# Attention and a two-layer network on one core: every product in 64x64 quarters of the matmul array, in an order worked out by a planner

## The chip, the core and the metric

The kernel runs on one core of a Trainium2 chip. A core has five engines with a queue each: TensorE (PE, matmuls; PEld is its weight load), VectorE (DVE), ScalarE (ACT), GpSimd (POOL) and SyncE (SP, which here only issues DMAs). They share the on-chip memory (SBUF, 128 partitions) and meet through semaphores; matmuls write to PSUM, eight banks of 512 f32 columns. Each engine takes its own instructions strictly in the order in which they were built. The metric is the device time of one execution in microseconds (us). The kernel before took 422.13 us, the median of two runs (421.86 and 422.4). A difference of about 2% is what counts as faster or slower here.

## The reference

Eight batches, twelve heads, 448 tokens, 64 channels a head; then a network of 768 -> 2048 -> 768 over the 3584 tokens.

```python
q_n, k_n = rmsnorm(q, g_q), rmsnorm(k, g_k)       # (8, 12, 448, 64)
scores = q_n @ k_n.T / sqrt(64);  attn = softmax(scores)
x = (attn @ v).transpose(0, 2, 1, 3).reshape(3584, 768)
out = gelu_tanh(x @ w_in) @ w_out                 # 768 -> 2048 -> 768
```

Inputs and output are f32; the kernels compute the products in bf16 with f32 sums.

## The kernel before

Per batch the work has a front (squares of q and k, their sums, one over the root, the normed tiles, a transpose to put channels on partitions), the attention, layer 1 and layer 2. Work of three batches runs at once: while batch b's scores and exponentials are made, layer 2 of earlier batches fills TensorE, and in layer 1 of batch b the front of batch b+1 runs on the other engines.

- **Scores** (`scores`, L300): for a pair of heads and 128 keys, one matmul a head, 64 rows by 128 columns of the array, the two heads side by side on the two row halves; the two outputs lie in two neighbouring PSUM banks, so that **one ACTIVATE (L326) takes the exponential of both heads, 896 columns**, with a per-partition bias `shift`. 448 keys are three blocks of 128 and a rest of 64; the rests of two pairs share one tile in four 64x64 matmuls (L310). A batch has 21 such tiles and so 21 exponentials.
- **Sums and products** (`pair_products`, L345): 128 rows by 64 columns, two heads on the two column halves. The rest block uses V tiles half filled with zeros (`vr`). DVE adds the exponentials of the key blocks (`key_sum`) before the sum product, and turns the sums into reciprocals (`recip_in`, `recip`, `recip_out`) and scales (`pair_x`).
- **Layer 1** (`mm1`) and **layer 2** (`mm2`): 128 rows by 64 columns, the two column halves one after the other (`parts=2`); the first batch's layer 1 and the last layer 2 tiles use the whole 128x128 array.
- **Front**: q is loaded with 4 tokens a partition on 112 partitions, k with 3 tokens a partition on 128 and a rest on 64. Transposes go through TensorE in the first batch and part of the second, later through DMA.

The order is written by hand: a string of steps for the first batch (`FRONT`, L737), and for the others lists of what comes after which group of layer 1 (`plan`, `first_blocks`) and how many layer 2 matmuls stand between two groups of scores (`FILLS`).

Of the kernel before, what the change touches and what calls it, by code (L numbers as in the profile page):

```python
# [12 lines left out]
AX = mybir.AxisListType  # L13


@with_exitstack
def kernel(
# [21 lines left out]
    P = 112  # L39
    NQ = S // P  # L40
    NK = 3
    NS = 7
    HP = H // 2
    CH = 4
    NCH = H // CH
# [3 lines left out]

    consts = ctx.enter_context(tc.tile_pool(name="consts", bufs=1))  # L50
    wts = ctx.enter_context(tc.tile_pool(name="wts", bufs=1))
    rawqk = ctx.enter_context(tc.tile_pool(name="rawqk", bufs=4))
    sqp = ctx.enter_context(tc.tile_pool(name="sqp", bufs=4))
    stp = ctx.enter_context(tc.tile_pool(name="stp", bufs=2))
    smp = ctx.enter_context(tc.tile_pool(name="smp", bufs=4))
    nrmp = ctx.enter_context(tc.tile_pool(name="nrmp", bufs=2))
    qkp = ctx.enter_context(tc.tile_pool(name="qkp", bufs=1))
    exq = ctx.enter_context(tc.tile_pool(name="exq", bufs=3))
    exr = ctx.enter_context(tc.tile_pool(name="exr", bufs=2))
    xp = ctx.enter_context(tc.tile_pool(name="xp", bufs=2))  # L60
    gp = ctx.enter_context(tc.tile_pool(name="gp", bufs=1))
    op = ctx.enter_context(tc.tile_pool(name="op", bufs=3))

    spots = [
        ctx.enter_context(tc.tile_pool(name=f"ps_s{i}", bufs=1, space=bass.MemoryType.PSUM))
        for i in range(2)
    ]
    unused, taken = [0, 1], []
    ps_o = ctx.enter_context(tc.tile_pool(name="ps_o", bufs=1, space=bass.MemoryType.PSUM))
    ps_m = ctx.enter_context(tc.tile_pool(name="ps_m", bufs=1, space=bass.MemoryType.PSUM))  # L70

    ps_t = tc.tile_pool(name="ps_t", bufs=1, space=bass.MemoryType.PSUM)
    ps_t_tiles = ps_t.__enter__()
# [5 lines left out]

    zeros = consts.tile([128, S], BF16)  # L80
    nc.vector.memset(zeros, 0.0)
    grow = consts.tile([D, 2], F32)
    for i, row in enumerate((g_q, g_k)):
        nc.scalar.dma_start(grow[:, i:i + 1], row.rearrange("(d o) -> d o", o=1))
    EXP_SET, GELU_SET = "natural_log_exp_and_others", "gelu_apprx_tanh_and_others"

# [5 lines left out]
    eps = consts.tile([128, 1], F32)  # L92
    win = wts.tile([128, HP, d_ff], BF16)
    wout = wts.tile([128, nf, d_model], BF16)

    vb = [wts.tile([128, H, NK, D], BF16, name=f"vb{i}") for i in range(2)]
    vr = [wts.tile([128, 2, HP, D], BF16, name=f"vr{i}") for i in range(2)]
    ones = consts.tile([128, D], BF16)
    onesr = consts.tile([128, 2, D], BF16)
    kT = consts.tile([128, NCH, NS, 128], BF16)  # L100

    NU = 4 * CH + 2 * NS
    ssq = [consts.tile([128, NCH, NU], F32, name=f"ss{i}") for i in range(3)]
    raws, sqs, rinvs, nrms = {}, {}, {}, {}
    qT, xT = {}, {}
    g = gp.tile([128, nf, 2 * S], BF16, tag="g", name="g")

    def slots(j):
        return slice(0, NK) if j == 0 else slice(NK, NS)

    def head(c, j):
        return 2 * c + HP * j

    def load_q(b, c):
        t = rawqk.tile([P, CH, NQ, D], F32, tag="rawq", name="rawq")
        raws["q", b, c] = t
        return [
            lambda j=j: nc.sync.dma_start(
                t[:, 2 * j:2 * j + 2],
                q[b, head(c, j):head(c, j) + 2].rearrange("h (p t) d -> p h t d", t=NQ),  # L120
            )
            for j in range(2)
        ]

    SM = 128 * NK

    def own(j):
        return slice(64 * j, 64 * j + 64)

    def load_k(b, c):  # L130
        t = rawqk.tile([128, 2, NS, D], F32, tag="rawk", name="rawk")
        raws["k", b, c] = t

        def main(j):
            h = head(c, j)
            nc.sync.dma_start(
                t[:, :, 4 * j:4 * j + NK],
                k[b, h:h + 2, :SM].rearrange("a (p t) d -> p a t d", t=NK),
            )

        def last(j):
            h = head(c, j)
            nc.sync.dma_start(t[own(j), :, NK], k[b, h:h + 2, SM:].rearrange("a p d -> p a d"))
        return [lambda: main(0), lambda: main(1), lambda: last(0), lambda: last(1)]

    def loads(b, c):
        lq, lk = load_q(b, c), load_k(b, c)
        for go in (lq[0], lk[0], lq[1], *lk[1:]):
            go()

    def load_v(b, part):
        if part == 0:
            nc.gpsimd.dma_start(
                vb[b % 2].rearrange("p h t d -> p h (t d)"),
                v[b, :, :SM].rearrange("h (p t) d -> p h (t d)", t=NK),
            )
        else:
            j = part - 1
            nc.gpsimd.dma_start(
                vr[b % 2][own(j), j], v[b, HP * j:HP * j + HP, SM:].rearrange("h p d -> p h d")  # L160
            )

    def view(n, t, j=None):

        if n == "q":
            return t if j is None else t[:, 2 * j:2 * j + 2]
        return t if j is None else t[:, :, slots(j)]

    def sq_tile(n, flat):
        if n == "q":  # L170
            return flat[:P].rearrange("p (h t d) -> p h t d", h=CH, t=NQ)
# [170 lines left out]
    def bank():  # L342
        return ps_o.tile([128, 512], F32, tag="o", name="o")
# [567 lines left out]
```

## Time and profile before

| | us |
|---|---|
| median of the runs | 422.13 |
| span of the profiled execution, first to last instruction | 418.5 |
| what lies around it, median less span | 3.6 |
| TensorE busy | 407.3 (97% of the span) |
| ScalarE / VectorE / GpSimd busy | 297.7 / 273.7 / 131.7 |
| matmuls | 4120, with as many weight loads |

Rows of the groups read: line, engine, operation, output<-inputs, rows\*columns of the array (for TensorE), shapes, count | busy us, mean ns of one | idle time of the engine ahead of it. Rows of the timeline read: start, length, engine, line, operation, tiles, count in a row. TensorE works in "passes" below: a pass is the time in which 448 (or 384) columns stream through the array once; several matmuls on different parts of the array share a pass.

### The profile page before, as it was taken

The page shows a single profiled execution, that of the slowest core. Times are in us where ns is not written, and L with a number is a line of the kernel's source. Part 1 is how long each engine was busy: PE and PEld are TensorE (multiplying, and loading weights), DVE is VectorE, ACT ScalarE, POOL GpSimd, SP SyncE. Part 2 cuts the span into 40 slices and gives each one's busy share as a digit, 9 for nine tenths or more (in the row PEclk, how much of TensorE's full clock was granted, in tenths as well). Part 3 has the DMA queues.
Part 4 walks back from the last instruction along what each step waited for, and adds up shares of the span by engine and source line. Part 5 has one row for each costly group of instructions (what it writes and reads, how often), then busy time and mean ns, then how long its engine had stood idle before and what let it go on. Part 6 is the DMA issues. An engine that isn't in the chain of part 4 may idle for free.

```text
span 418.5 us, 9913 instructions
## 1 busy us (share of the span) xinstructions
PE 407.3 (97%) x4120; PEld 249.6 (60%) x4120; DVE 273.7 (65%) x454; ACT 297.7 (71%) x401; POOL 131.7 (31%) x142
## 2 busy tenths in 40 slices
PE   7899899999999999999999999999999999999996
PEld 3244455576655765567655765567655675557664
DVE  5898758899589648881678747786578642782010
ACT  4897787879997787776967778685876558774300
POOL 7897400033200744037500745019500560000000
PEclk9699999999999999999999999999999999999999
DMA  7999999938981499419881398718681161210022
GB/s 191 217 231 230 204 198 228 237 108 178 219 143 39 75 212 199 95 44 187 205 143 39 74 205 156 146 39 158 152 142 39 26 109 40 67 49 0 2 78 76
DMA packets 97870, 54.20 MB, mean 130 GB/s; under 512 B 63776, under 2 KB 94368, under 8 KB 97824
## 3 DMA queue, kind: packets, MB, share of 16 engines
q1 hardware_dynamic: 71424, 41.71, 42.2%
q0 software_dynamic: 26112, 11.80, 22.2%
q8 instruction: 32, 0.52, 0.5%
q14 instruction: 14, 0.11, 0.1%
q10 hardware_dynamic: 288, 0.06, 0.1%
HBM read 45.61 MB, written 11.01 MB: 135 GB/s over the span
## 4 chain that ended last, share of the span: by engine, by line
PE 91%; DVE 4%; ACT 3%; issue 1%; ACTq 0%; DVEq 0%
PE o L436 33%; PE hh L407 29%; PE o L365 12%; PE sc L320 7%; PE h L407 4%; PE sc L310 2%; ACT ex L326 1%; PE w L217 1%; PE ox L365 1%; DVE nrmq L226 1%; DVE nrmk L226 1%; PE o L472 1%; PE tp L238 0%; DVE qT L255 0%; DVE kT L264 0%
## 5 line engine op out<-in xcount | busy, mean ns | idle before, releaser
L436 PE MATMUL o<-wout,g 128*64 128x384 bf16 (+1 forms) x1648 | 155.3, 326 | 0.0
L326 ACT ACTIVATE ex<-sc,shift 128x896 bf16<-128x896 f32 x144 | 135.8, 1012 | 1.7 <-PE sc L320 1.6
L407 PE MATMUL hh<-xT,win 128*64 128x448 bf16 (+1 forms) x1260 | 133.2, 353 | 0.0
L407 PEld LDWEIGHTS <-win 128*64 128x64 bf16 (+1 forms) x1440 | 102.4, 109 | 42.4 <-issue 0.8
L436 PEld LDWEIGHTS <-g 128*64 128x64 bf16 (+1 forms) x1648 | 97.2, 109 | 47.8 <-issue 3.8
L416 ACT ACTIVATE g<-hh 128x896 bf16<-128x896 f32 x56 | 49.9, 918 | 40.6 <-PE hh L407 40.6
L203 DVE TENSOR_REDUCE ss<-sq 128x14 f32<-128x896 f32 (+4 forms) x45 | 47.7, 1081 | 31.7 <-ACT sq L186 20.1
L449 ACT COPY osb<-o 128x384 f32<-128x384 f32 x51 | 24.6, 483 | 50.0 <-PE o L436 49.9
L764 POOL COPY mark<-es 1x1 bf16<-1x1 bf16 x7 | 1.7, 242 | 166.1 <-DVE es L340 152.6
L372 DVE STREAM_TRANSPOSE st<-o 128x448 f32<-128x448 f32 x48 | 31.1, 648 | 25.3 <-PE o L365 25.2
L320 PE MATMUL sc<-qT,kT 64*128 64x448 bf16 x288 | 39.1, 359 | 2.5 <-DVE kT L264 1.5
L340 DVE TENSOR_TENSOR es<-ex 128x896 bf16<-128x896 bf16 x42 | 26.6, 632 | 15.9 <-ACT ex L326 15.9
L226 POOL TENSOR_TENSOR nrmq<-rawq,rinv 112x512 bf16<-112x512 f32 x34 | 35.2, 1050 | 2.8 <-ACT rinv L212 2.6
L380 DVE STREAM_TRANSPOSE rb<-rc 128x448 f32<-128x448 f32 x48 | 31.0, 645 | 1.6
L365 PE MATMUL o<-ex,vb 128*64 128x448 bf16 x252 | 31.2, 353 | 0.1
L226 POOL TENSOR_TENSOR nrmk<-rawk,rinv 128x512 bf16<-128x512 f32 (+1 forms) x33 | 30.9, 952 | 0.0
L279 DVE TENSOR_SCALAR kT<-kT,gcol 128x896 bf16<-128x896 bf16 x19 | 19.6, 1032 | 12.4 <-DMA kT<-nrmk 12.4
L338 DVE TENSOR_TENSOR es<-es,exr 64x896 bf16<-64x896 bf16 x42 | 25.9, 617 | 2.7 <-ACT exr L326 1.3
L340 DVE TENSOR_TENSOR es<-es,ex 128x896 bf16<-128x896 bf16 x42 | 25.6, 609 | 2.7 <-ACT ex L326 0.8
L188 POOL TENSOR_TENSOR sq<-rawq 112x1024 f32<-112x1024 f32 x9 | 17.6, 1951 | 30.9 <-DMA rawq<-in_q_dram 17.4
L390 DVE TENSOR_TENSOR xT<-o,rb 128x448 bf16<-128x448 f32 x42 | 25.9, 616 | 0.9 <-PE o L365 0.4
L320 PEld LDWEIGHTS <-kT 64*128 64x128 bf16 x288 | 10.0, 94 | 24.9 <-issue 17.8
(83 smaller groups left out, 347.2 us busy)
## 6 DMA issues: line engine op xcount, KB each, us to landing
rawq<-in_q_dram SPq DMA_DIRECT2D x48, 224.0 KB, 4.4
rawk<-in_k_dram SPq DMA_DIRECT2D x48, 192.0 KB, 4.6
vb<-in_v_dram POOLq DMA_DIRECT2D x8, 576.0 KB, 11.6
win<-in_moe_w_in_dram POOLq DMA_DIRECT2D x4, 768.0 KB, 14.1
wout<-in_moe_w_out_dram POOLq DMA_DIRECT2D x4, 768.0 KB, 20.2
out_dram<-osb SPq DMA_DIRECT2D x7, 336.0 KB, 3.3
out_dram<-osb SPq DMA_DIRECT2D x8, 288.0 KB, 2.7
out_dram<-osb SPq DMA_DIRECT2D x8, 240.0 KB, 2.5
```

The source lines that it names most:

```text
L203: nc.vector.reduce_sum(stat(ssq[b % 3], b, c, n, j), view(n, sqs[n, b, c], j), axis=AX.X)
L226: eng.tensor_mul(dst.rearrange("p t a d -> p a t d"), view(n, raws[n, b, c], j), r.to_broadcast(list(r.shape) + [D]),)
L320: nc.tensor.matmul(sc[:, a, :S], kT[r, c, 4 * j + t], qT[b][r, hp], start=True, stop=True,)
L326: nc.scalar.activation(dst, sc[:, :, :S], AF.Exp, scale=scale, bias=shift)
L338: nc.vector.tensor_add(es[p], es[p], exrs[b, hp // 2][p])
L340: nc.vector.tensor_add(es, ex[:, 0] if t == 1 else es, ex[:, t])
L365: nc.tensor.matmul(o[a * D:(a + 1) * D], w(a), e[:, a], start=(i == 0), stop=(i + 1 == len(steps)),)
L372: nc.vector.transpose(oas["st"].rearrange("p a b -> p (a b)"), oas[0])
L380: nc.vector.transpose(oas["rb", hp], oas["rc"].to_broadcast([128, S // 32, 32]))
L407: nc.tensor.matmul(h[i * m:(i + 1) * m, j, :S], win[:, c // 2 + NCH * (c % 2), f * 128 + i * m:f * 128 + (i + 1) * m], xT[b][:, c], start= ...
L416: nc.scalar.activation(g[:, fs[0]:fs[0] + len(fs), (b % 2) * S:(b % 2 + 1) * S], hs1[fs[0]][:, :, :S], AF.Gelu_apprx_tanh)
L436: nc.tensor.matmul(o[j * m:(j + 1) * m, :HD], g[:, f, i * 128 + j * m:i * 128 + (j + 1) * m], wout[:, f, half * HD:(half + 1) * HD], start ...
```

## The change

The kernel is written anew. What differs:

- **Every product is made of 64x64 matmuls.** The array is used as two row halves ("ways" R0 and R1), each with two column quarters. A step is two matmuls, one for each column quarter, on one way; two ways with a step each fill the array. Twice as many matmuls are issued: 8273 in place of 4120.
- **One PSUM bank at a time.** All eight banks are single tiles, and the code never lets the two ways write one bank at once. Scores of the two heads go to two single banks, so **the exponential is of 448 columns, 42 a batch in place of 21**. In layers 1 and 2 a bank is filled by one way's rows first and then by the other's: the first matmul of the second half waits until the last of the first half has written (`after_own`), 128 times in layer 1 and 56 times in layer 2.
- **7 tokens a partition** for q, k, v and the output: no rest block; loads are of 1792 bytes a row and head, two heads on 64 partitions. The first chunk is loaded and prepared one head at a time (`BY_HEAD`). The loads of k for it are issued from ACT's queue.
- **A planner** (`Plan`) orders all steps: each has an engine, a cost, what it depends on and a rank; the lists are then issued in the order of the planned starts. The planner's numbers hold 450 ns for an exponential, 190 and 163 ns for a step of layer 1 and layer 2.
- Sums: DVE adds seven key blocks of 896 columns (two heads) as before; the first batch sums on TensorE. Output tiles are copied out by ACT and DVE in turn. Layer 2 ends with ordinary tiles.

```diff
+    def score(b, n, a):
+        c, t = divmod(n, NT)
+        scs[a, n] = sc = bank("sc")
+        for j in range(2):
+            nc.tensor.matmul(
+                sc[own(j), :S].rearrange("p (t s) -> p t s", t=NT),
+                kT[own(a), c, t, own(j)], qT[own(a), c, :, own(j)], start=True, stop=True,
+            )
+    def exp(b, n, a):
+        c, t = divmod(n, NT)
+        sc = scs.pop((a, n))
+        nc.scalar.activation(
+            exs[b, c][:, t, a], sc[:, :S], AF.Exp, scale=scale, bias=shift)
+        leave(sc)
+    def layer1(b, f, r, first, i):
+        if first and i == 0:
+            hs[f] = bank("hh")
+        elif i == 0:
+            after_own(lasts["h", f])
+        c, j = divmod(i, 2)
+        for m in range(2):
+            at = f * 128 + m * 64
+            lasts["h", f] = nc.tensor.matmul(
+                hs[f][own(m), :S], win[own(r), c + NCH * j, at:at + 64], xT[b][own(r), c, j],
+                start=(first and i == 0), stop=(not first and i == HP - 1),
+            )
+    def layer2(u, h, r, first, f):
+        if first and f == 0:
+            ops[u, h] = bank("oq")
+        elif f == 0:
+            after_own(lasts["o", u, h])
+        i = u % NT
+        for m in range(2):
+            at = i * 128 + m * 64
+            lasts["o", u, h] = nc.tensor.matmul(
+                ops[u, h][own(m), :HD], g[own(r), f, at:at + 64],
+                wout[own(r), f, h * HD:(h + 1) * HD],
+                start=(first and f == 0), stop=(not first and f == nf - 1),
+            )
...
+    SLOT, SLOT2 = (190, 356), (163, 329)
+        exp=(450, 566), gelu=(428, 543), table=(1283, 1283), rsqrt=(620, 680), evictA=(365, 478),
...
-        def exp():
-            nc.scalar.activation(dst, sc[:, :, :S], AF.Exp, scale=scale, bias=shift)
-            leave(sc)
...
-                    nc.tensor.matmul(
-                        h[i * m:(i + 1) * m, j, :S],
-                        win[:, c // 2 + NCH * (c % 2), f * 128 + i * m:f * 128 + (i + 1) * m], xT[b][:, c],
-                        start=(c == 0), stop=(c == HP - 1),
-                    )
```

Three places show how instructions stand. The first is ScalarE's queue where batch 4's attention begins: `g` are layer 1's outputs (L416 before, L491 now), the table load switches from gelu to exp, `ex` and `exr` are the exponentials, and `osb` is a copy of a layer 2 tile. Before:

```order
L416 ACTIVATE g<-h 128x448 [waits PE_49]
L868 ACT_TABLE_LOAD
L326 ACTIVATE ex<-sc,shift 128x896 [waits DVE_49,PE_49]
L326 ACTIVATE ex<-sc,shift 128x896 [waits PE_49] x2
L449 COPY osb<-o 128x384 [waits PE_49]
L326 ACTIVATE ex<-sc,shift 128x896 [waits DVE_49,PE_49]
L326 ACTIVATE ex<-sc,shift 128x896 [waits PE_49]
L326 ACTIVATE exr<-sc,shift 128x896 [waits PE_49]
L449 COPY osb<-o 128x384 [waits PE_49] x2
```

Now, to the end of that attention:

```order
L491 ACTIVATE g<-hh 128x448 [waits PE_49] x2
L566 ACT_TABLE_LOAD
L419 ACTIVATE ex<-sc,shift 128x448 [waits DVE_49,PE_49]
L419 ACTIVATE ex<-sc,shift 128x448 [waits PE_49] x8
L516 COPY osb<-oq 128x384 [waits DMAHW3_49,PE_49]
L419 ACTIVATE ex<-sc,shift 128x448
L419 ACTIVATE ex<-sc,shift 128x448 [waits PE_49] x4
L419 ACTIVATE ex<-sc,shift 128x448 [waits DVE_49,PE_49]
L419 ACTIVATE ex<-sc,shift 128x448 [waits PE_49] x12
L516 COPY osb<-oq 128x384 [waits PE_49]
L419 ACTIVATE ex<-sc,shift 128x448
```

The exponentials are half as wide and twice as many; of seven copies of layer 2 tiles in one attention, two are left on this queue.

The second place is TensorE's queue in the middle of an attention (batch 4 before, batch 3 now): a tile of scores `sc` and the layer 2 matmuls beside it (`o` before, `oq` now; each matmul has its weight load ahead of it). Before, with the key sums between:

```order
L320 LDWEIGHTS kT
L320 MATMUL sc<-qT,kT 128x448 [waits Activation_49]
L320 LDWEIGHTS kT
L320 MATMUL sc<-qT,kT 128x448
L365 LDWEIGHTS ones [waits DVE_49]
L365 MATMUL o<-es,ones 64x448 [waits Activation_49]
L365 LDWEIGHTS ones
L365 MATMUL o<-es,ones 64x448
L436 LDWEIGHTS g
L436 MATMUL o<-wout,g 64x384 [waits Activation_49]
```

Now, with the numbers of the tiles, which tell the two open layer 2 banks apart (one is filled by R0, the other by R1):

```order
L411 LDWEIGHTS kT_130
L411 MATMUL sc_4207<-qT_131,kT_130 64x448 [waits Activation_49]
L411 LDWEIGHTS kT_130
L411 MATMUL sc_4207<-qT_131,kT_130 64x448
L505 LDWEIGHTS g_135
L505 MATMUL oq_4117<-wout_127,g_135 64x384
L505 LDWEIGHTS g_135
L505 MATMUL oq_4117<-wout_127,g_135 64x384
L505 LDWEIGHTS g_135
L505 MATMUL oq_4117<-wout_127,g_135 64x384
L505 LDWEIGHTS g_135
L505 MATMUL oq_4117<-wout_127,g_135 64x384
```

A score is now one step on one way, and single scores alternate with a few layer 2 steps, where three tiles of scores stood together between 14 to 48 layer 2 matmuls.

The third place is the head of ScalarE's queue, with the loads of the gains (`grow`), of k, and the first use of the gains. Before:

```order
L84 DMA grow<-in_g_q_dram 64x1
L84 DMA grow<-in_g_k_dram 64x1
L585 ACT_TABLE_LOAD
L626 ACTIVATE gcol<-grow 64x1 [waits DMAHW2_49,DMAHW0_49]
L626 ACTIVATE gcol<-grow 64x1
```

Now:

```order
L566 ACT_TABLE_LOAD
L682 DMA grow<-in_g_q_dram 64x1
L682 DMA grow<-in_g_k_dram 64x1
L316 DMA raw<-in_k_dram 64x448
L316 DMA raw<-in_k_dram 64x448 [waits DMAHW0_49]
L316 DMA raw<-in_k_dram 64x448 [waits DMAHW1_49]
L316 DMA raw<-in_k_dram 64x448 [waits DMAHW3_49]
L545 ACTIVATE gcol<-grow 64x1 [waits DMAHW4_49,DMAHW2_49]
```

The table load stands ahead of the loads, and the loads of k, which were SyncE's, stand behind it, three of them with a wait for an earlier load.

More of the change, by code (lines that the diff above doesn't have):

```diff
@@ L68 @@
[L68 to L73, printed above, removed]
+        ctx.enter_context(tc.tile_pool(name=f"ps{i}", bufs=1, space=bass.MemoryType.PSUM))
+        for i in range(8)
+    ]
+    unused, taken = list(range(8)), []
     ident = consts.tile([128, 128], BF16)
@@ L125 @@
[L125 to L144, printed above, removed]
@@ L884 @@
+    nc.vector.memset(eps, 1e-6)
+    nc.vector.memset(ones, 1.0)
+    nc.vector.memset(rows, 1.0)
+    w = bank("w_")
+    for _ in range(20):
+        nc.tensor.matmul(w[:, :S], zeros[:, :128], zeros, start=True, stop=True)
+    leave(w)
+    PL.run()
+    PL.issue()
 _INS = ['q', 'k', 'v', 'g_q', 'g_k', 'moe_w_in', 'moe_w_out']
```

1201 lines of the change are left out of this document (549 added, 652 removed).

## The prediction

> **What bounds the kernel now.** First the page's busy times, then the granted clock, then the stretches of one batch (engines in the order PE, PEld, DVE, ACT, POOL; then clock, DMA share, GB/s):
>
> ```profile
> span 418.5 us, 9913 instructions
> PE 407.3 (97%) x4120; PEld 249.6 (60%) x4120; DVE 273.7 (65%) x454; ACT 297.7 (71%) x401; POOL 131.7 (31%) x142
> PEclk9699999999999999999999999999999999999999
> PE 91%; DVE 4%; ACT 3%; issue 1%; ACTq 0%; DVEq 0%
> 103.30:152.10 48.80, 48.58 (x527) 30.93 (x528) 36.64 (x58) 40.15 (x57) 14.75 (x17) 1.00 0.68 132
> 248.80:297.10 48.30, 48.30 (x526) 30.58 (x525) 33.66 (x51) 36.40 (x50) 17.61 (x18) 1.00 0.65 133
> ```
>
> TensorE is the bound: 91% of the chain that ended last, never idle in a middle batch, at full clock. A batch takes 48.3 us, and ScalarE has 12 us to spare in it. Only what shortens TensorE's list can gain, and only until another engine's list is as long. The timeline of TensorE in batch 4, then the durations of line L310 (least, median and most of the 96, in ns) and four rows of the chain, show what the list is made of:
>
> ```profile
> 200.53 0.74 PE L320 MATMUL sc<-qT,kT 64*128 64x448 bf16 x6
> 201.20 4.09 PE L436 MATMUL o<-wout,g 128*64 128x384 bf16 x48
> 205.22 0.55 PE L320 MATMUL sc<-qT,kT 64*128 64x448 bf16 x4
> 205.70 0.38 PE L310 MATMUL sc<-qT,kT 64*64 64x448 bf16 x4
> 206.02 4.09 PE L436 MATMUL o<-wout,g 128*64 128x384 bf16 x48
> ...
> L310 PE MATMUL sc<-qT,kT x96: 347/373/578, 13.0 to 368.5; 64*64 64x448 bf16 x96
> ...
> 102.19 1.14 PE h L407 x12
> 238.61 9.14 PE hh L407 x96
> 392.61 1.13 PE h L407 x12
> 393.74 18.31 PE o L436 x112
> ```
>
> A layer 1 pass (two matmuls side by side) takes 9.14/48 = 0.190 us, a layer 2 pass of 384 columns 18.31/112 = 0.1635. From the four quarter matmuls of L310 to the next group are 0.32 us, from the four of L320 ahead (two passes) 0.48: where the shape changes, a pass costs some 0.1 us more.
>
> **The change, part by part.** *TensorE's passes.* Before, a batch has 96 passes of layer 1, 21 of scores, 24 of products, 6 of sums, all at 0.190, and 112 of layer 2: 27.9 + 18.3 = 46.2 us; the 2.1 us left of 48.3 are the changes of shape, some 20 at 0.1. Now there is one shape, products are 21 and sums 3: 26.8 + 18.3 = 45.1 us. So the change takes 3.2 us a batch off TensorE, if a pass of four quarters costs what one of two matmuls does. No stream of quarters is in the trace. The nearest row is L310: four within 0.38 us, where one alone lasts 0.373 (its line's median), so they start within 10 ns of each other and run at once; I take 0.190 and 0.1635. The upper end is the fastest long run of load and matmul pairs, two in 0.1635 us, 0.082 each: four would take 0.327, and 2042 such passes over 660 us in all.
>
> *ScalarE in the attention.* The rows of groups for exp and gelu, then ScalarE's timeline at the start of batch 4:
>
> ```profile
> L326 ACT ACTIVATE ex<-sc,shift 128x896 bf16<-128x896 f32 x144 | 135.8, 1012 | 1.7 <-PE sc L320 1.6
> L416 ACT ACTIVATE g<-hh 128x896 bf16<-128x896 f32 x56 | 49.9, 918 | 40.6 <-PE hh L407 40.6
> L416 ACT ACTIVATE g<-h 128x448 bf16<-128x448 f32 x16 | 8.8, 549 | 1.5 <-PE h L407 1.5
> ...
> 199.26 1.33 PE L407 MATMUL h<-xT,win 128*64 128x448 bf16 x12
> ...
> 200.78 0.54 ACT L416 ACTIVATE g<-h 128x448 bf16<-128x448 f32 x1
> 201.33 1.28 ACT L868 ACT_TABLE_LOAD   x1
> 202.62 2.80 ACT L326 ACTIVATE ex<-sc,shift 128x896 bf16<-128x896 f32 x3
> 205.31 0.49 ACT L449 COPY osb<-o 128x384 f32<-128x384 f32 x1
> 205.67 1.94 ACT L326 ACTIVATE ex<-sc,shift 128x896 bf16<-128x896 f32 x2
> ```
>
> Three exponentials in a row take 2.80, so one starts (2.80 - 1.01)/2 = 0.895 us after another. Gelu shows what half the columns save: 918 - 549 = 369 ns, not half of 918. An exponential of 448 columns then comes every 0.895 - 0.369 = 0.525 us, and 42 take 22.05 us where 21 took 18.8. The bounds are 0.448 (half) and 0.643 (1.012 - 0.369, no overlap), which would make a leg A below 4.6 us longer still; I take 0.525, since both its numbers are rows.
>
> In the Trainium skill, "ScalarE: Activation LUTs", section "What ACT_TABLE_LOAD costs", an ACTIVATE with a pointer bias takes 280 ns + 0.833 a column, less 93 of overlap. That is 1026 for 896 columns (the trace has 1012) and 560 from start to start for 448; by it the sum below would be some 10 us longer. The fixed part agrees with the trace's in kind.
>
> This decides the legs of a batch. **Leg A** runs from the last layer 1 matmul of the batch ahead to the last score. ScalarE must finish the gelu and switch tables (200.59 to 202.62: 2.0 us), do 39 exponentials before the last of 42 scores finds one of three score banks free (39 x 0.525 = 20.5), and two copies (205.31 to 205.67, 0.36 each): **23.2 us**. TensorE's list in that leg has 82 to 87 layer 2 steps and 36 others on its busier way, 87 x 0.1635 + 36 x 0.19 = 21.0 us: it stands still for 2.2 us. **Leg B** runs from there to the last layer 1 matmul: ScalarE has 16 gelus at 0.55, four squares of about 1, a square root and a table load of 1.28, under 15 us, and TensorE sets the end. Its busier way has, for batches 2 to 7, 106, 104, 106, 104, 106, 104 steps at 0.190 and 49, 22, 49, 22, 31, 27 of layer 2: 28.1 + 23.4 + 28.1 + 23.4 + 25.2 + 24.2 = 152.4 us. Six batches: 6 x 23.2 + 152.4 = **291.6 us**. Before, from 102.19 + 1.14 to 392.61 + 1.13: **290.4**. The 3.2 us a batch are eaten by leg A's 2.2 and by ways that are not equally long.
>
> *Handing a bank from way to way.* 184 times a weight load waits for a matmul some places ahead in the same queue; while it waits, both ways stand behind it. A matmul ends 0.353 after its start, and gelu starts 0.19 after the modelled end of the matmuls (200.59 to 200.78): 0.54 us. Between stand mostly 6 to 8 steps of both ways, 0.57 to 0.76 us from start to start; nine handoffs of layer 2 have two or three, at 0.1 us each. I take nothing; if the spare fails, all pay 0.1: 18 us.
>
> *Start and first two batches.* The rows at the start, and the end of the first attention and layer 1:
>
> ```profile
> 1.19 0.46 SPq L136 DMA_DIRECT2D rawk<-in_k_dram  x1
> 1.33 0.62 ACTq L84 DMA_DIRECT2D grow<-in_g_k_dram  x1
> 1.98 1.28 ACT L585 ACT_TABLE_LOAD   x1 [1.98 <-issue]
> 4.26 0.86 DVE L188 TENSOR_TENSOR g<-rawk 128x384 f32<-128x384 f32 x1 [2.84 <-DMA rawk<-in_k_dram]
> 11.05 2.98 ACT L326 ACTIVATE ex<-sc,shift 128x896 bf16<-128x896 f32 x3
> 22.57 0.33 ACT L209 ACTIVATE lg<-ss,eps 128x14 f32<-128x14 f32 x1
> 22.93 0.21 ACT L212 ACTIVATE rinv<-lg 128x14 f32<-128x14 f32 x1
> 23.15 1.01 ACT L326 ACTIVATE exr<-sc,shift 128x896 bf16<-128x896 f32 x1
> 31.36 2.82 ACT L326 ACTIVATE ex<-sc,shift 128x896 bf16<-128x896 f32 x3
> 53.25 2.43 PE L407 MATMUL h<-xT,win 128*128 128x448 bf16 x12
> ```
>
> k used to be usable 3.1 us after its issue at 1.19. Now table load and gains go ahead of it, and its second half waits for an earlier load: issued about 3.7, usable 6.8. The first exponential then starts near 12; the second needs the other head's front, which stands behind two reductions in DVE's queue. I let the exponentials run through from 15.0 (12 to 16): 42 x 0.525 + 0.6 for a square root between them (22.57 to 23.15) + 0.1 to the last one's end is 37.8, against 34.18 before (31.36 + 2.82). With the same 21.5 us from there to the end of layer 1 (53.25 + 2.43 = 55.68 before) that is 59.3, **3.6 late**. Batch 1: leg A 23.2 again, where TensorE has but 16.4 us of steps; leg B 112 steps and 47 of layer 2, 29.0; so 111.5 against 103.33, 4.5 more.
>
> *The end.* Layer 2 left over is 142 steps on the busier way, 23.2 us (its last half chain runs alone), then 0.16 to the end of the matmul, 0.56 for the copy and 3.5 for the store, as here:
>
> ```profile
> 414.73 0.27 ACT L477 COPY osb<-o 128x128 f32<-128x128 f32 x1 [2.12 <-PE o L472]
> ```
>
> (to the span's end at 418.5). 27.4 against 418.5 - 393.74 = 24.8.
>
> *At nothing,* with two rows of the page:
>
> ```profile
> L188 POOL TENSOR_TENSOR sq<-rawk 128x896 f32<-128x896 f32 x7 | 11.7, 1678 | 0.0
> wout<-in_moe_w_out_dram POOLq DMA_DIRECT2D x4, 768.0 KB, 20.2
> ```
>
> DVE's, GpSimd's and the DMAs' work changes in shape, not much in size. DVE has 33.7 of 48.3 us. The next batch's six norms on GpSimd take 6 x 1.7 = 10 us and their transposes go by DMA, all within leg B's 23; without that cover the next scores would be late by what they overrun. The first layer 2 chain, near 61, needs all of `wout`; its four loads are issued right behind those of `win`, by 36 or so, and land 20 us later. Should they be late, TensorE has 6.8 us to spare in that leg.
>
> **Sum:** 59.3 + 52.2 + 291.6 + 27.4 = 430.5, against the profiled 418.5. With the 3.6 that lie around it (422.13 - 418.5): **434 us**, 2.8% slower.
>
> **Rivals.** *Exponentials cost half.* If the fixed part overlaps wholly, 0.448 us each: leg A falls to TensorE's 21.0, 13.2 less over six batches, 3.0 in batch 1 and 3.2 in the first: 434 - 19.4 = 414.6, faster by 1.8%. It decides below 0.468 us, where ScalarE needs 21.0. For it: their rows overlap by 0.117 already. Against: gelu's two rows.
>
> *TensorE cannot be fed.* Four loads and four matmuls a pass need a pair every 0.041 us in layer 2 and 0.0475 in layer 1, twice the rate of any long run here. From there the pass grows with the pair: at 0.05, 2.3 us more in a leg B, 1.3 in a leg A, 5.2 at the end, 31 in all: 465 us. For it: nothing in the trace reaches that rate for long. Against: L310's four in 10 ns.
>
> The Trainium skill's "TensorE: Matmul & The Clock Gate", section "Wait — 56ns, not 53.3ns?", gives a floor of 25 ns between starts, and 62 ns a matmul where firmware decodes. The 62 would make a pass 0.248 and the whole over 540; L310's 10 ns for four are under both figures, but only for a burst.
>
> *Handoffs stall*: the 18 us above, 452.
>
> **Chances.** The forecast (424 to 444: the start 3 us either way, the exponential between 0.50 and 0.55): 0.50. Half-cost exponentials (404 to 424, with the same spread): 0.22. Unfed TensorE 0.15, handoffs 0.13. Half of the second case lies below 413.7, 2% faster; 2% is about what a measurement of this kernel can tell from no change: faster 0.11. Same is its other half and a fifth of the forecast, below 430.6: 0.22. Slower 0.67. The range leaves out a tenth at each end, the faster half of the second case and the dearer halves of the last two: 413 to 456.
>
> **What would show it.** In the profile after: exponentials 0.52 us apart and TensorE waiting for `ex` by some 2 us a leg A; layer 2 runs at 0.163 us for four matmuls; first exponentials run through from 15; layer 1 of batch 1 ends near 111. Steps closer than 0.47 us, or four quarters taking over 0.2, would make me wrong, down or up.

## The result, and the profile after

The changed kernel takes **492.75 us** (median of two runs, 491.69 to 493.81) against 422.13: 1.168 times as long, 95% interval 1.161 to 1.174. The forecast was 434, the range 413 to 456. Its profiled execution took 493.8, with a span of 492.0. The lines of the page that answer to those of before:

```profile
span 492.0 us, 18274 instructions
PE 439.2 (89%) x8273; PEld 324.8 (66%) x8273; DVE 281.3 (57%) x445; ACT 299.9 (61%) x559; POOL 131.0 (27%) x95
PE   5778997959999699997999699998999699999995
PEclk9595999987999899997999899997999889999999
PE 44%; ACT 26%; DVE 14%; DMA 7%; issue 4%; POOL 2%; SPq 1%; DVEq 0%; ACTq 0%; POOLq 0%
```

TensorE holds 44% of the chain that ended last, where it held 91%. Its row of busy tenths has a hole in each of batches 1 to 6 and none in batch 7, and the granted clock dips at or behind each hole. Two stretches are set side by side, each from the last layer 1 matmul to the last score (leg A) and on to the next last layer 1 matmul (leg B): those of batch 2 and of batch 7, the last one. Columns as before: PE, PEld, DVE, ACT, POOL, granted clock, DMA share, GB/s.

```profile
135.62:159.09 23.47, 22.51 (x463) 17.89 (x459) 15.61 (x30) 23.22 (x45) 1.11 (x2) 1.00 0.40 76
159.09:194.57 35.48, 30.27 (x624) 24.76 (x618) 20.75 (x26) 15.66 (x28) 15.79 (x10) 0.95 0.73 132
415.44:439.18 23.74, 22.65 (x488) 18.32 (x483) 15.38 (x31) 23.56 (x46) 0.00 (x0) 1.00 0.15 37
439.18:463.58 24.40, 24.40 (x529) 21.80 (x524) 7.43 (x15) 10.59 (x20) 0.00 (x0) 1.00 0.08 19
```

Leg A is as forecast in both, 23.5 and 23.7 us against 23.2. Leg B of batch 7 is too: 24.40 against 24.2, with TensorE busy throughout. Leg B of batch 2 took 35.48 against 28.1. What tells the two apart is the last column of engines: in batch 2 GpSimd works 15.8 us, in batch 7, which has no next batch to prepare, not at all.

The timelines of GpSimd, VectorE and TensorE in that leg B show what happens (start, length, engine, line, operation; in brackets what ended the wait):

```profile
161.72 7.79 POOL L364 TENSOR_TENSOR nrm<-raw,rinv 128x896 bf16<-128x896 f32 x4 [24.98 <-issue]
...
159.50 0.58 DVE L429 TENSOR_TENSOR es<-ex 128x896 bf16<-128x896 bf16 x1
160.00 0.62 DVE L469 TENSOR_TENSOR xT<-xo,rb 128x448 bf16<-128x448 f32 x1
160.54 7.42 DVE L429 TENSOR_TENSOR es<-es,ex 128x896 bf16<-128x896 bf16 x5
...
161.34 2.46 PE L505 MATMUL oq<-wout,g 64*64 64x384 bf16 x52
168.02 0.38 PE L436 MATMUL so<-es,ones 64*64 64x448 bf16 x4 [4.22 <-DVE es L429]
168.23 1.68 PE L505 MATMUL oq<-wout,g 64*64 64x384 bf16 x26
169.57 0.58 PE L461 MATMUL xo<-ex,vb 64*64 64x448 bf16 x2
```

The last exponential ends at 161.0. Five additions of the key sums (L429) take 7.42 us, three of them 1.92 each, just while four norms of the next batch run on GpSimd. TensorE runs out of layer 2 steps, stands still for 4.2 us until the sums are there, and then takes 0.58 for a matmul that took 0.35. Over the whole kernel, first the durations of line L429 (least, median and most of the 105, in ns), then the row of the waits for the sums (us in all, times, longest):

```profile
L429 DVE TENSOR_TENSOR es<-es,ex x105: 582/625/1995, 80.9 to 442.3; 128x896 bf16<-128x896 bf16 x105
```

```profile
PE so L436 <- DVE es L429: 29.9, 13, 6.5
```

Seventeen additions last 1.92 to 1.99 us, 22.4 us more than at 0.62 each; none of them is in batch 7.

In the sum of the prediction the miss of 61.5 us (span 492.0 against 430.5) stands as follows. The times are the ends of the last layer 1 matmuls; the last two columns are two kernels of the experiments.

| stage | forecast | changed kernel | `hold_sq` | `comb` |
|---|---|---|---|---|
| start to the end of batch 0's layer 1 | 59.3 | 72.0 | 70.5 | 66.3 |
| batch 1 | 52.2 | 64.0 | 55.2 | 56.1 |
| batches 2 to 7 | 291.6 | 328.0 | 298.3 | 299.4 |
| the rest | 27.4 | 28.1 | 28.4 | 28.1 |
| median of the runs | 434 | 492.75 | 455.8 | 451.9 |

### The profile page after: what moved, and what is told of

It reads as the page before. It is cut to its first block, busy times and chain, and to the rows that moved or that the text cites. A ratio compares the mean times of both kernels' runs of the same rounds, so it can differ in the third digit from the quotient of the medians.

```text
span 492.0 us, 18274 instructions
## 1 busy us (share of the span) xinstructions
PE 439.2 (89%) x8273; PEld 324.8 (66%) x8273; DVE 281.3 (57%) x445; ACT 299.9 (61%) x559; POOL 131.0 (27%) x95
## 4 chain that ended last, share of the span: by engine, by line
PE 44%; ACT 26%; DVE 14%; DMA 7%; issue 4%; POOL 2%; SPq 1%; DVEq 0%; ACTq 0%; POOLq 0%
ACT ex L419 21%; PE hh L484 21%; PE oq L505 12%; DVE es L429 10%; PE xo L461 6%; PE sc L411 3%; DMA raw<-in_q_dram 2%; PE so L436 2%; DMA kT<-nrm 2%; POOL nrm L364 2%; ACT L566 2%; DMA qT<-nrm 1%; DMA raw<-in_k_dram 1%; ACT g L491 1%; ACT osb L516 1%
## 5 line engine op out<-in xcount | busy, mean ns | idle before, releaser
L505 PE MATMUL oq<-wout,g 64*64 64x384 bf16 x3584 | 224.8, 331 | 0.1
L419 ACT ACTIVATE ex<-sc,shift 128x448 bf16<-128x448 f32 x336 | 181.5, 788 | 12.0 <-PE sc L411 11.9
L505 PEld LDWEIGHTS <-g 64*64 64x64 bf16 x3584 | 156.0, 109 | 28.7 <-issue 2.9
L484 PE MATMUL hh<-xT,win 64*64 64x448 bf16 x3072 | 162.8, 351 | 2.4 <-ACT g L491 1.5
L484 PEld LDWEIGHTS <-win 64*64 64x64 bf16 x3072 | 121.1, 107 | 32.2 <-issue 6.7
L491 ACT ACTIVATE g<-hh 128x448 bf16<-128x448 f32 x128 | 62.7, 541 | 122.4 <-PE hh L484 122.3
L364 POOL TENSOR_TENSOR nrm<-raw,rinv 128x896 bf16<-128x896 f32 (+1 forms) x40 | 73.1, 1851 | 184.6 <-issue 138.6
L411 PE MATMUL sc<-qT,kT 64*64 64x448 bf16 x672 | 114.5, 370 | 3.9 <-DVE qT L391 3.6
L429 DVE TENSOR_TENSOR es<-es,ex 128x896 bf16<-128x896 bf16 x105 | 88.0, 838 | 18.7 <-ACT ex L419 13.3
L461 PE MATMUL xo<-ex,vb 64*64 64x448 bf16 x672 | 72.6, 408 | 0.4
L436 PE MATMUL so<-es,ones 64*64 64x448 bf16 x84 | 11.6, 414 | 30.2 <-DVE es L429 29.9
L444 DVE STREAM_TRANSPOSE st<-so 128x448 f32<-128x448 f32 x48 | 28.6, 629 | 15.6 <-PE so L436 15.6
L469 DVE TENSOR_TENSOR xT<-xo,rb 128x448 bf16<-128x448 f32 x48 | 28.6, 616 | 8.7 <-PE xo L461 8.2
L516 ACT COPY osb<-oq 128x384 f32<-128x384 f32 x28 | 15.6, 557 | 24.2 <-PE oq L505 20.1
```

The lines of the kernel that those rows point to most:

```text
L364: ENG[eng].tensor_mul(dst, half(raws[b, c][:, n], a), r.to_broadcast(list(r.shape) + [D]))
L411: nc.tensor.matmul(sc[own(j), :S].rearrange("p (t s) -> p t s", t=NT), kT[own(a), c, t, own(j)], qT[own(a), c, :, own(j)], start=True, sto ...
L419: nc.scalar.activation(exs[b, c][:, t, a], sc[:, :S], AF.Exp, scale=scale, bias=shift)
L429: nc.vector.tensor_add(es, ex[:, 0] if t == 1 else es, ex[:, t])
L436: nc.tensor.matmul(sos[b, c, j][own(a), :S], ones[own(j)], e[own(j), a], start=(t is None or t == 0), stop=(t is None or t == NT - 1),)
L444: nc.vector.transpose(sts[x].rearrange("p a b -> p (a b)"), sos[x][:, :S])
```

## The experiments

Theories: **the lock** (the norms on GpSimd and the additions on VectorE take turns at the memory, and the change took away what kept them apart); **the late order** (the planner's list has additions behind the last exponential, because it prices an exponential at 450 ns); **the clock** (the stop itself costs, since TensorE is slower after it).

**Hold the norms back (`hold`).** The kernel before had a one-element copy on GpSimd (L764, `mark<-es`) that waits for the last addition of a batch. Its batch 4, VectorE and then GpSimd:

```profile
232.23 0.63 DVE L340 TENSOR_TENSOR es<-es,ex 128x896 bf16<-128x896 bf16 x1
...
232.92 0.18 POOL L764 COPY mark<-es 1x1 bf16<-1x1 bf16 x1 [23.99 <-DVE es L340]
233.06 2.04 POOL L226 TENSOR_TENSOR nrmq<-rawq,rinv 112x512 bf16<-112x512 f32 x2
```

The addition ends, the copy goes, and only then the norms start. The new planner says only that a norm comes `after` the start of that addition in its plan; on the chip nothing waits: in batch 2 of the changed kernel the first norm starts at 161.72, 0.14 us behind its root, and that addition at 166.04. The copy is put back:

```diff
+            add(name("mark", b), "POOL", lambda b=b: nc.gpsimd.tensor_copy(
+                mark, ess[b, NCH - 1][0:1, 0, 0:1]), (150, 200),
+                deps=[name("add", b, NCH * NT - 1)], rank=200 * b + 60)
...
-        return [f"add.{b - 1}.20"] if b > 1 else []
+        return [f"mark.{b - 1}"] if b > 1 else []
```

> One thing is put back that the kernel before had: GpSimd copies one element of the last key sum of a batch (a wait for VectorE's last addition) before it starts the next batch's norms. Lock theory: in the changed kernel 17 additions of key sums (L429) take 1.92 to 1.99 us instead of 0.62 while a norm runs on GpSimd, 22.4 us in all, because the two engines take turns at the memory, one whole instruction each; TensorE stands still behind them and its granted clock then drops (0.65 for 4.9 us in batch 2). With the norms held back no addition takes over 0.7, TensorE's wait for the key sums falls from 29.9 us to under 6, and the time from 492.7 to about 458 (22 for the locks, some 11 for the clock). Late-order theory (the additions are late because the planner's list has four of them behind the last exponential, whatever GpSimd does): those four still come behind it, so the time stays within 2% of 492.7.

Measured: **465.8 us**, 1.098 (1.090 to 1.107) times the kernel before, 27 less than the changed kernel. The durations of its additions, then the timeline of VectorE and GpSimd in batch 2, then TensorE's waits:

```profile
L429 DVE TENSOR_TENSOR es<-es,ex x105: 583/625/628, 80.8 to 415.5; 128x896 bf16<-128x896 bf16 x105
```

```profile
153.64 3.53 DVE L429 TENSOR_TENSOR es<-es,ex 128x896 bf16<-128x896 bf16 x5
...
157.41 6.63 POOL L364 TENSOR_TENSOR nrm<-raw,rinv 128x896 bf16<-128x896 f32 x4
```

```profile
PE hh L484 <- ACT g L491: 7.0, 7, 1.7
PE so L436 <- DVE es L429: 6.7, 11, 1.0
```

All seventeen are back at 0.62, though their order on VectorE is the same and they still stand behind the last exponential. The late order alone doesn't make the loss. The time fell 8 us less than expected: TensorE now waits 7.0 us in layer 1 for gelu, where it waited 1.5.

**Half norms (`halves`).** The same collision with shorter instructions on GpSimd:

```diff
-        ENG[eng].tensor_mul(dst, half(raws[b, c][:, n], a), r.to_broadcast(list(r.shape) + [D]))
+        for i in (0, 1) if b > 1 else (a,):
+            r = stat(rinvs[b], b, c, n, i)
+            dst = half(nrms[b, c][:, n].rearrange("p t a d -> p a t d"), i)
+            ENG[eng].tensor_mul(dst, half(raws[b, c][:, n], i), r.to_broadcast(list(r.shape) + [D]))
```

> Every norm of batches 2 to 7 on GpSimd is split into two instructions of 448 columns (0.93 us each in the first batch), started at the same moment as before, so they still lie beside the additions. Lock by whole instructions: an addition then waits for half a norm, and takes 1.2 to 1.3 us in place of 1.92; the time falls by about 12 us for the 17 additions and some 4 for a shorter stop of TensorE, to about 477. Shared bandwidth (both engines simply run slower beside each other): the additions keep their 1.92 and the time stays at 492. Late-order theory: also 492.

Measured: **473.0 us** (ratio 1.111 to 1.123). The durations of its additions (L430 here), then the timeline of the same five in batch 2 and of GpSimd:

```profile
L430 DVE TENSOR_TENSOR es<-es,ex x105: 581/625/1244, 79.9 to 422.6; 128x896 bf16<-128x896 bf16 x105
```

```profile
156.72 5.17 DVE L430 TENSOR_TENSOR es<-es,ex 128x896 bf16<-128x896 bf16 x5
...
157.90 8.37 POOL L365 TENSOR_TENSOR nrm<-raw,rinv 128x448 bf16<-128x448 f32 x8 [25.31 <-issue]
```

The slow additions take 1.11 to 1.24 us in place of 1.92: an addition lasts about as long as the GpSimd instruction beside it, whatever its own size. Had the two engines shared a bandwidth, the length of GpSimd's instructions would not matter. The single instructions say the same: in the changed kernel a norm runs from 163.39 to 165.45 and an addition from 164.01 to 165.93, here a half from 158.82 to 160.13 and an addition from 159.44 to 160.61. In both runs every slow addition ends 0.48 us behind the end of the norm that was running when it started. The norms pay as well, 1.31 for a half that takes 0.93 alone.

The Trainium skill has this rule, in "SBUF — State Buffer", section "Who interferes with whom": a VectorE instruction with two SBUF inputs contends with a GpSimd instruction that reads SBUF. The section "Summary: rules for kernel authors" of the same page adds that the second one to issue is blocked until the first finishes. Both runs agree, 1.92 and 1.17 us for an addition that takes 0.62 alone. VectorE's transposes (L444) and its multiplications by `rb` (L469), which have at most one input in SBUF, took no more than 0.65 us beside the same norms in the changed kernel.

**Fill the gap (`filler`).** Matmuls ahead of the last sum, their result overwritten:

```diff
+        for _ in range(16 if 0 < b < 7 and c == NCH - 1 and j == 0 else 0):
+            for a in range(2):
+                nc.tensor.matmul(
+                    sos[b, c, j][own(a), :S], ones[own(j)], exs[b, c][own(j), 0, a],
+                    start=True, stop=True,
+                )
```

> 32 matmuls more (16 steps of the key sum on one way, their result overwritten) stand ahead of the last sum product of batches 1 to 6, 192 in all, about 3.0 us a batch, where TensorE stands still for 2.4 to 6.5 us. Clock theory: the stop itself is what lowers the granted clock afterwards (0.65 in batch 2 for 4.9 us, which costs 1.7); with the gap filled the clock stays near 1.0 and the time falls by 6 to 11 us, to 482 to 487, although work is added. If the stop does not set the clock, the time stays at 492.7, or rises by up to 3 where the gap is shorter than the filling.

Measured: **489.3 us** (ratio 1.148 to 1.161), 3.4 less than the changed kernel with 192 matmuls more; the two intervals touch, so the gain is barely clear of the noise. The stretches of 5 us behind the wait of batch 2 and of batch 4, first in the changed kernel, then in this one (the granted clock is the third number from the end):

```profile
168.00:173.00 5.00, 4.98 (x76) 3.70 (x80) 3.72 (x8) 0.00 (x0) 1.51 (x1) 0.66 0.10 20
...
279.80:284.80 5.00, 5.00 (x62) 3.39 (x66) 3.32 (x7) 0.00 (x0) 1.44 (x1) 0.50 0.02 3
```

```profile
167.00:172.00 5.00, 5.00 (x80) 4.30 (x83) 3.72 (x8) 0.00 (x0) 1.42 (x1) 0.66 0.05 12
...
278.00:283.00 5.00, 5.00 (x116) 4.07 (x112) 4.98 (x10) 0.00 (x0) 1.25 (x1) 1.00 0.28 70
```

In batch 4 the dip is gone and 116 matmuls are done in place of 62; in batch 2 it stays, though only 1.4 us of the stop are left. So the stop does lower the clock, but filling on one way doesn't always hold it up. In the changed kernel the clock stands at 0.50 for 6.8 us in leg B of each of batches 3 to 6; here it stays at 1.00 there, and those legs are 1.9, 1.1, 1.1 and 2.7 us shorter. The clock is the small part, and the expected 6 to 11 us were too much.

**The price alone (`exp525`).**

```diff
-        exp=(450, 566), gelu=(428, 543), table=(1283, 1283), rsqrt=(620, 680), evictA=(365, 478),
+        exp=(525, 640), gelu=(428, 543), table=(1283, 1283), rsqrt=(620, 680), evictA=(365, 478),
```

> One number of the planner is changed: an exponential is given 525 ns (640 to its end) in place of 450 (566), as the trace of the changed kernel has it. The lists that come out have one addition behind the last exponential in batches 2 to 6, where the changed kernel's have five or three, and still five in batch 1. Late-order theory: the wrong price is the cause of the late additions, and most of batch 2 to 6's loss goes: 17 additions at 1.3 us less 4 in batch 1, so 17 us, and the clock's 9 with them, to about 466; the collisions of batch 1 stay. Lock theory: the same, since no addition is left to lie beside a norm, and 466 as well; it differs only in batch 1, where it expects four additions near 2 us. If instead the price was right and the order doesn't matter, the time stays at 492.

Measured: **477.6 us** (ratio 1.122 to 1.133), more than either theory said. Six additions stay slow: four in batch 1 (1.3 to 1.9 us), and one each in batches 3 and 5, which still have two behind the last exponential. Legs B of batches 2 to 7 fall to 165.3 us in all from 187.6, but legs A rise to 150.3 from 140.3, since the new lists put more layer 2 into them: some 2310 of its matmuls in place of 1950, which at 0.041 us each (0.1635 for four) is 14 to 15 us of work moved out of legs B and of what follows them. An order with the right price avoids most collisions by chance, not by rule.

**The root of the start (`start`).** The timeline of ScalarE in the first attention of the changed kernel:

```profile
14.59 0.63 ACT L419 ACTIVATE ex<-sc,shift 128x448 bf16<-128x448 f32 x1 [1.16 <-PE sc L411]
...
18.80 2.21 ACT L419 ACTIVATE ex<-sc,shift 128x448 bf16<-128x448 f32 x4 [0.72 <-PE sc L411]
21.53 1.16 ACT L419 ACTIVATE ex<-sc,shift 128x448 bf16<-128x448 f32 x2 [0.53 <-PE sc L411]
23.28 11.12 ACT L419 ACTIVATE ex<-sc,shift 128x448 bf16<-128x448 f32 x21 [0.59 <-PE sc L411]
34.14 0.47 ACT L356 ACTIVATE lg<-ss,eps 128x28 f32<-128x28 f32 x1
34.64 0.23 ACT L357 ACTIVATE rinv<-lg 128x28 f32<-128x28 f32 x1
43.79 7.45 ACT L419 ACTIVATE ex<-sc,shift 128x448 bf16<-128x448 f32 x14 [8.92 <-PE sc L411]
```

The squares' sums for the third pair group are ready at 24.4 (VectorE's last reduction of it starts at 23.30 and takes 1.07), but its root stands behind 28 exponentials, at 34.14.

```diff
-             (0, 2, 3, None, 50, []), (1, 0, 1, None, 95, ["exps.0"]),
+             (0, 2, 3, None, -1, []), (1, 0, 1, None, 95, ["exps.0"]),
```

> One rank of the planner is changed: the root of the first batch's third pair group (the ACT rows lg and rinv at 34.14 in the changed kernel) gets rank -1 instead of 50, and so stands after some 11 exponentials of the first attention and not after 28. Theory of the start: the 8.9 us in which ScalarE waits for a score at 34.9 come from that place, since the norms, transposes and scores of the group all follow the root; with it moved the gap goes, the first attention ends near 43.5 in place of 51.2, layer 1 of the first batch near 64 in place of 72, and the time falls by 7 to 9 us, to about 484. Rival: GpSimd and VectorE, which make these norms behind loads and reciprocals, or the loads themselves, are late anyway; then the gap shrinks by 2 us at most and the time stays at 491 to 493. The later batches' lists change a little too; their legs should stay within 2 us.

Measured: **475.8 us** (ratio 1.123 to 1.129). In its timeline the row that had the wait of 8.92:

```profile
37.06 7.70 ACT L419 ACTIVATE ex<-sc,shift 128x448 bf16<-128x448 f32 x14 [1.93 <-PE xo L461]
```

The first attention ends 6.5 us earlier (44.8), layer 1 of batch 0 at 66.8 in place of 72.0: 5.2 us. The other 12 us are not the start's. The new lists also moved the later batches: in batch 1 no addition lies beside a norm any more (5.9 us less), in batches 2 and 3 three in place of five. The expectation that the later legs stay within 2 us was wrong, and the total would have misled without the stages.

**The squares (`hold_sq`).** The timeline of ScalarE in layer 1 of batch 2, in `hold`:

```profile
166.49 0.98 ACT L491 ACTIVATE g<-hh 128x448 bf16<-128x448 f32 x2 [0.16 <-PE hh L484]
170.87 0.95 ACT L337 ACTIVATE sq<-raw 128x896 f32<-128x896 f32 x1 [3.40 <-DMA raw<-in_k_dram]
171.72 0.53 ACT L491 ACTIVATE g<-hh 128x448 bf16<-128x448 f32 x1
173.33 0.95 ACT L337 ACTIVATE sq<-raw 128x896 f32<-128x896 f32 x1 [1.08 <-DMA raw<-in_q_dram]
174.19 1.83 ACT L491 ACTIVATE g<-hh 128x448 bf16<-128x448 f32 x4
```

A square waits for its load with gelus behind it. The edit, on top of `hold`:

```diff
-        return "ACT" if c < 2 else "POOL"
+        return "ACT" if c < 1 else "POOL"
```

> The kernel with the norms held back, and the squares of the second pair group of batches 3 to 7 on GpSimd in place of ScalarE. Theory of the queue: with the norms held back, TensorE still waited 7.0 us in layer 1 for gelu (7 times, up to 1.7 us), because ScalarE stood at a square whose q or k had not been loaded yet, with the gelus behind it in its queue; the loads come late because their buffers are freed by the norms. Without these squares on ScalarE the wait falls below 2 us, the clock does not drop after it, and the time goes from 465.8 to about 457. Rival: the gelus are late for the matmuls' own sake (banks handed from way to way); then the wait stays at 7 and the time within 2 us of 465.8. GpSimd gets 2 x 1.68 us more a batch, in a stage where it has some 10 us free, which should cost nothing.

Measured: **455.8 us** (ratio 1.075 to 1.083), 10 less than `hold`. TensorE's wait for gelu is no longer among its waits, the granted clock of batch 2's leg B is 1.00, and the leg is 28.85 us, against 33.05 in `hold` and 28.1 forecast. The stretches of leg B of batch 2 and leg A of batch 3:

```profile
148.84:177.69 28.85, 28.52 (x622) 26.25 (x616) 16.32 (x25) 13.88 (x26) 17.01 (x12) 1.00 0.80 144
177.69:200.78 23.09, 22.65 (x486) 17.36 (x478) 16.75 (x33) 22.67 (x43) 1.16 (x2) 1.00 0.50 103
```

| leg B of batch | 2 | 3 | 4 | 5 | 6 | 7 | sum |
|---|---|---|---|---|---|---|---|
| forecast | 28.1 | 23.4 | 28.1 | 23.4 | 25.2 | 24.2 | 152.4 |
| changed kernel | 35.5 | 29.7 | 35.9 | 29.7 | 32.4 | 24.4 | 187.6 |
| `hold` | 33.1 | 27.1 | 30.2 | 26.8 | 25.8 | 24.4 | 167.5 |
| `hold_sq` | 28.9 | 25.1 | 28.9 | 25.1 | 25.8 | 24.4 | 158.1 |

**All three (`comb`).** `hold_sq` with the early root.

> The three edits together: norms held back, squares of the second group on GpSimd, the early root. If the three losses are separate, they add: 465.8 less 9 less 8, about 449. If they hide each other, it stays above 455. The forecast of 434 for the changed kernel would be missed by 15 still: a leg B that starts with three additions and the reciprocals behind the last exponential, 3 us in each of six batches.

Measured: **451.9 us** (ratio 1.066 to 1.076). The start's part adds less than expected, 4 us: layer 1 of batch 0 ends 4.2 earlier than in `hold_sq`, at 66.3, and batch 1 is 0.9 longer.

**Sums on TensorE instead of a hold (`comb_pe`).** With the early root and the squares on GpSimd, the last additions are taken away rather than guarded:

```diff
-    PE_SUMS = {(0, 0), (0, 1), (0, 2)}
+    PE_SUMS = {(0, 0), (0, 1)} | {(b, 2) for b in range(B)}
...
-        return [f"add.{b - 1}.20"] if b > 1 else []
+        return [f"exps.{b - 1}"] if b > 1 else []
```

> In place of holding the norms back, the additions beside them are taken away: the key sums of every batch's third pair group are made on TensorE from the seven exponential tiles, as the first batch does it (six steps more a way and batch, 6 x 0.190 = 1.14 us, 8 us in seven batches); with the early root and the squares on GpSimd. Lock theory: with no addition left behind the last exponential, the norms may start right there and slow nothing: no addition over 0.7 us, and the sums are ready about 1.5 us behind the last exponential instead of 3.2 (held) or 7 (changed kernel). That gains 1.7 us over the held version in seven legs B, and costs 1.14 in each: about 445. If it is not the additions but the norms' own traffic that slows the stage, the time stays above 460.

Measured: **453.9 us** (ratio 1.071 to 1.077). The output of this version is not the reference's, for a cause that was not found; its time is read for where the work stands, not as a way to go. Norms start 0.7 us behind the last exponential, no addition lies beside one, and none is over 0.63 us. That agrees with the lock theory without testing it again; the norms' own traffic as the cause (over 460) is out. The time is 9 us above the expected 445. Batches 2 to 7 fall to 284.8 us, 14.6 below `comb`, but what follows them rises from 28.1 to 43.6, as layer 2 that had filled waits is left for the end (912 of its matmuls in place of 532). In legs B of batches 2 to 7 TensorE then waits for 0.4 us in all: its list is the sum there again.

**Price and hold together (`comb525`).** The edits of `comb` and of `exp525`.

> The three edits of the version before (norms held back, squares on GpSimd, early root), and the planner's price of an exponential at 525 in place of 450. Theory that what is left in leg B is the additions behind the last exponential: with one or two of them instead of three or four, legs B of batches 2 to 6 become 1 to 1.5 us shorter each; but with that price alone legs A were 25.0 us in place of 23.4. So 449 to 455, no gain over the 451.9 without it. If the wrong price were the root of the loss, it would fall to 440 or less.

Measured: **452.75 us** (ratio 1.069 to 1.073), as expected. Legs A are 150.7 us in place of 141.3, legs B 147.7 in place of 158.0. Legs B hold some 330 layer 2 matmuls fewer, 13.5 us of work, and legs A some 340 more. With nothing colliding, the planner's price mainly moves layer 2 from one leg to the other.

**The wait taken out of the kernel before (`before_nomark`).**

```diff
-        nc.gpsimd.tensor_copy(mark, x)
+        pass
```

> The kernel before, without its seven one-element copies on GpSimd (L764) that make it wait for a batch's last key addition. In its batch 4 the root of the next batch is ready at 231.55, the last addition runs from 232.23 to 232.86, and the norms (1.04 us each here) start at 233.06. Lock theory: without the copies a norm starts at 231.6, and the last addition, alone of its kind so late, takes up to 1.7 us instead of 0.63; the key sums come 1 us later in each of five or six batches, where TensorE has layer 1 matmuls to do in between, so the time rises by 1 to 6 us, to 423 to 428: one addition is beside a norm there, not two to four. If the copies are what the two kernels differ by in full, it rises by 20 us or more; if the lock isn't there, it stays at 422.5.

Measured: **431.2 us**, 1.0195 (1.0175 to 1.0215) times the kernel before, clear of the noise but just at the 2% that counts. The durations of its additions, then its timeline in batch 4:

```profile
L340 DVE TENSOR_TENSOR es<-es,ex x42: 582/618/2287, 62.2 to 388.2; 128x896 bf16<-128x896 bf16 x42
```

```profile
238.46 2.33 POOL L226 TENSOR_TENSOR nrmq<-rawq,rinv 112x512 bf16<-112x512 f32 x2 [25.68 <-issue]
...
239.00 2.28 DVE L340 TENSOR_TENSOR es<-es,ex 128x896 bf16<-128x896 bf16 x1
...
241.34 0.38 PE L365 MATMUL o<-es,ones 128*64 128x448 bf16 x2 [1.26 <-DVE es L340]
```

In four batches (3 to 6) one addition lasts 2.28 or 2.29 us: it waits out two of the norms here, one after the other. In batch 1 another, of 2.10, lies beside a square on GpSimd. TensorE waits 1.26 us for the one shown, and a middle batch takes 49.7 us in place of 48.3. The wait that the change dropped was worth 8.5 us even there, more than the 1 to 6 expected. In the changed kernel two to four additions meet norms that are longer.

## Why the prediction was wrong

- **Passes of four quarters cost 0.190 and 0.1635 us: right.** Two long runs in the timeline of the changed kernel:

```profile
447.01 15.25 PE L484 MATMUL hh<-xT,win 64*64 64x448 bf16 x316
463.74 23.25 PE L505 MATMUL oq<-wout,g 64*64 64x384 bf16 x532
```

  15.25/79 = 0.193 and 23.25/133 = 0.175, the last chains alone included; the forecast for that last stretch was 23.2. The rival that TensorE cannot be fed is out, and so is the pass of 0.248 that the prediction set beside its own.
- **An exponential every 0.525 us, leg A 23.2: right.** Eighteen in a row take 0.517 each (143.15 to the copy at 152.45 in batch 2). Six legs A sum to 140.3 against 139.2, batch 1's is 23.15. The half-cost rival is out, and the dearer 0.560 that the prediction set beside its price is not borne out.
- **Handoffs cost nothing: right** by batch 7, whose leg B holds sixteen handoffs of layer 1 and is 0.2 us over its list.
- **The end, 27.4: right** (28.1).
- **"The next batch's six norms on GpSimd take 6 x 1.7 = 10 us and their transposes go by DMA, all within leg B's 23": the step that failed.** The 10 us were hidden as time on GpSimd, but not as use of the memory: each addition beside them waited for a norm to end and lost 1.3 us by it (22.4 us in 17 additions). The prediction even gave the price of the cover's loss as an overrun of the norms; what was lost was the other engine's work. And it passed over the removed copy (L764), a wait of 23.99 us on GpSimd in the profile of before. In the six batches, holding the norms back takes away 20.1 of the 36.4 us missed (328.0 to 307.9), in batch 1 it takes 6.7 of 11.8.
- **"ScalarE has 16 gelus at 0.55, four squares of about 1 [...] under 15 us, and TensorE sets the end": the second step that failed.** Its time was nearly right (15.7 us in batch 2, which takes in the last exponentials), its order wasn't: a square that waits for its load holds up the gelus behind it. In `hold`, where loads come later still, this costs 9.6 us of six batches. How much of it the changed kernel pays with the norms unheld was not separated: its own wait there is 1.5.
- **"I let the exponentials run through from 15.0": wrong, 12.7 us.** 4.2 (`comb` against `hold_sq`) to 5.2 (`start`) are the root behind 28 exponentials, which the order showed and the prediction did not look up. Most of the 7.5 left in `start` are shorter waits seen there: 3.2 for the second head (18.72 less one exponential, not 15.0), and 0.87, 0.59 and 1.93 behind it; these were read from rows, not tried.
- **What is left** of 61.5 us in `comb` is 19.4: 7.0 at the start, 3.9 in batch 1, 7.8 in batches 2 to 7, 0.7 at the end. Of the 7.8, legs B hold 5.6 and legs A 2.2. Whether the three or four additions that still follow the last exponential make those in legs B is open: with one or two of them (`comb525`) legs B fall by 10.3 us, but 13.5 us of layer 2 work has left them.

The sign was right for small reasons (of 12 us, 3.6 at the start, 4.5 in batch 1, 1.2 in the six batches, 2.6 at the end), and the size came from what was costed at nothing; that the kernel came out slower does not confirm the sum. No version of the new kernel here beats the kernel before.

## To carry to other kernels

Hidden work is free only if it uses nothing that the work above it uses: look for the engine that shares the memory with it, not just for the one whose time it is in. Before a wait is dropped, ask what it kept apart; a planner's order is no wait, and on the chip an engine starts as soon as its own inputs are there. Judge an edit to an automatic order by stages, since one rank can move the lists of batches far behind it.

## What the runs showed of the hardware beyond this

- Two engines in turn: beside norms of 1.69 us an addition of 0.62 takes 1.92 and the norm 2.06; beside halves of 0.93, 1.17 and 1.31. Both lose, and VectorE the more, the longer GpSimd's instruction is. From one norm's start to the next are 2.03 us, with halves 1.27: both times 0.28 less than the two instructions take alone. The turns are not always one each: in `before_nomark` an addition waited out two norms of 1.04 and took 2.28.
- In a dense run the exponentials start every 0.517 us while each is recorded at 0.79 us on the mean (L419), longer than the 0.63 of one alone: start to start, not duration, is the price in a row.
- After a stop of 4.2 us in batch 2 the granted clock was 0.66 on the mean of 5 us, and so it was after one of 1.4 us that 3 us of matmuls on one way had shortened; in batch 4 the same filling and the same stop left it at 1.00. The Trainium skill's "TensorE: Matmul & The Clock Gate", section "HAM oscillation — how this bites in real kernels", puts the limit at idle gaps of about 3.4 us; the first stop agrees. A shorter one is no safety here: in batches 3 and 5 of the changed kernel TensorE stood still for 2.46 us with nothing filled in, and the clock was 0.50 from 223.7 to 230.5 and from 336.3 to 343.1. What decides it below that limit is not shown.
